# New order and engine choices for the first 330 steps of a linear-attention kernel with a gated convolution

## The chip, the cores and the metric

The kernel runs on one core of a Trainium2 chip. The core has five engines, each with its own queue of instructions that it works through in order: TensorE (PE in the profile; its weight loads are shown as PEld and overlap its matmuls), VectorE (DVE), ScalarE (ACT), GpSimd (POOL) and SyncE (SP), which here only issues transfers. Transfers run on 16 DMA engines and are issued from the queues of SP, GpSimd and ScalarE. [...]

The metric is the device time of the whole program in microseconds (us), as the median of several runs. Lower is better.

## The reference

```python
def _attn_ref(q, k, v, w_phi):          # q, k, v: 8 x 8 x 576 x 64; w_phi: 64 x 128
    def phi(x):
        proj = np.einsum('bhsd,df->bhsf', x, w_phi)
        proj = proj - np.max(np.abs(proj), axis=-1, keepdims=True)
        return np.concatenate([np.exp(proj), np.exp(-proj)], axis=-1)
    q_p, k_p = (phi(q), phi(k))
    kv = np.einsum('bhsf,bhsd->bhfd', k_p, v)
    z = np.sum(k_p, axis=2)
    num = np.einsum('bhsf,bhfd->bhsd', q_p, kv)
    den = np.einsum('bhsf,bhf->bhs', q_p, z)[..., None] + 1e-06
    return num / den

def _moe_ref(x, w_val, conv_w, w_out):  # x: 8 x 576 x 512, the attention's heads side by side
    gate_pre[t] = sum over k < 5 of conv_w[k] * x[t - 4 + k]     # causal, zeros ahead of the start
    gate = 1 / (1 + np.exp(-gate_pre))
    return gate * (x @ w_val) @ w_out
```

The output is 8 x 576 x 512 in float32.

## The kernel before

**Steps.** The work is one list of 1062 numbered steps, made by `build` (from L163) as a loop over the 8 batches. A step is some instructions of one kind on one engine. Within a batch the 18 column blocks of 128 of q and of k are cut into five units (`UNITS`, L24): four of four blocks and a short one of two, here called the first to the fifth block of k or of q. The steps of one batch are these:

- The k and q of batch 0 are loaded as float32 by SP in pieces (`load32`, L520 to L527), transposed on PE (`tp32`, L533 to L536) and copied out of PSUM as bf16 by VectorE or ScalarE (`tc32`, L538 to L544). Batch 1 is loaded by GpSimd as bf16 and transposed on PE (`tp16` and `tc16`, L552 to L562); from batch 2 on, the transposes are DMAs (`xpose`, L564 to L567).
- `kp` and `qm` project k and q with the weights W2 (`proj`, L570 to L578). VectorE takes the largest absolute value of each row (`amax`, L583 to L587; maxima of k go to MK, of q to MQP), and ScalarE takes exp(+x) and exp(-x) of the projected k into KTIL (`kexp`, L593 to L598).
- ScalarE makes exponentials of the maxima of k (`ek`, L600 to L604), GpSimd multiplies V by them (`vs`, L606 to L611), PE sums k's features times V (`st`, L613 to L622), and `kv` copies that out.
- The maxima of q are transposed (`mqt`), negated (`mqr`), spread out into RX by GpSimd (`rx`, L673 to L685) and subtracted inside the second projection of q (`qp`, L687 to L699); ScalarE takes its exponentials into QTIL (`qexp`, L701 to L710).
- `num` multiplies by KV, `nrm` divides (L713 to L741), `xtp` and `xtc` transpose the result, `gate` and `val` are the convolution and the value matmuls (L772 to L792), `tanh` and `gv` gate, `out` multiplies by the output weights, `oev` copies out and `odma` stores.

**The order.** Nothing is scheduled while the kernel runs. Four strings written out by hand at the top of the file set everything: `ORDER` is the order of the steps, and so the order on each engine's queue; `FLEX` has one letter for each step that could go to more than one engine (A for ScalarE, D for VectorE, P for GpSimd); `BANKS` has the PSUM banks of each group of steps, and a group can begin only when the group that had its bank before has been read out; `WARM` and `ZERO` place idle matmuls ahead of positions of `ORDER`. `Plan.follow` (L147 to L156) reads the first three. The durations given with the steps in `build` don't reach the program.

**Idle matmuls.** `warm` (L490) multiplies ones by ones into a bank that nobody reads. `zero` (L493 to L505) adds a product with zeros to a bank that holds a result, which leaves the result as it is.

**The weights of the projection.** `c_w` (L451 to L456) is called while the tiles are made, so it stands ahead of all steps. Its two loads and the load of the convolution's weights are issued from ScalarE's queue; VectorE casts W32 to W2 at L455.

**The hold.** `hold` (L507 to L509) is a one-column copy on GpSimd that reads the last piece of q of batch 0. It stands on GpSimd's queue ahead of the loads of batches 1 and 2 (`load`, L546 to L550), so that they are issued when that piece has landed. `holdx` does the same for later batches.

Of the kernel before, what the change touches and what calls it, by code (L numbers as in the profile page):

```python
# [19 lines left out]
P = 128  # L20
# [15 lines left out]
    "0:5:10:256 13:5:2:512 60:6:1:512 81:1:1:512 87:7:2:512 134:7:1:512 141:7:1:512 "  # L36
)
ZERO = "35:76:7 61:80:5 75:34:1 101:105:1 126:215:8 144:223:1 155:192:4 158:200:1 175:315:6 189:346:1 195:241:2 197:241:2 211:327:1"
# [41 lines left out]
)  # L80
FLEX = (
    "AAAAAADAAADDPPPPDDDDAADDDDDDDDDDDDDAAADAAAADDDDAAADDDAADAAADDADAADDDDADDDDADDDDDDAADADDAAAAAA"
)
BANKS = (
    "037362307001454523232323016701676714232367230101676012354423010145454501013660564675601456745010145450101676767014501454"
# [279 lines left out]
class Emit:  # L365
# [85 lines left out]
    def c_w(self):  # L451
        nc = self.nc
# [37 lines left out]
    def warm(self, bank, n):  # L490
        self.nc.tensor.matmul(self.PS[:, bank, 0:n], self.ONES[:, 0:P], self.ONES[:, 0:n], start=True, stop=True)

    def zero(self, t):  # L493
        w = UNITS[t.u][1] * P
# [345 lines left out]
def kernel(  # L840
# [11 lines left out]
    nc = tc.nc  # L852
# [48 lines left out]
```

## Time and profile before

| | |
|---|---|
| time, median of 3 runs | 216.12 us (216.04 to 216.87) |
| the profiled execution's own time | 215.82 us |
| its span, first to last instruction | 214.1 us |
| PE busy | 195.6 us (91%), 3936 matmuls |
| VectorE busy | 170.3 us (80%) |
| ScalarE busy | 180.3 us (84%) |
| GpSimd busy | 132.6 us (62%) |
| granted TensorE clock, mean | 0.994 |
| moved by DMA | 39.92 MB |

How to read it: a row of the timeline gives start, duration, engine, line of the kernel, operation, output and inputs, and in brackets the idle time of that engine just before it and what ended it. Rows of one kind that follow closely are merged (x2). An engine's name with a q behind it is its queue issuing a transfer. A matmul's duration holds its way through the array, so PE can be busy without being at its peak. The granted clock is the share of full speed that PE was given; it is recorded from 6.6 us on, and where nothing is recorded the views print 1.00.

### The profile page before, as it was taken

How to read it: one execution, taken by the hardware profiler on the slowest of the kernel's cores; microseconds unless marked ns; L12 is line 12 of the kernel's file. 1: busy time of each engine (PE TensorE's matmuls, PEld its weight loads, DVE VectorE, ACT ScalarE, POOL GpSimd, SP SyncE). 2: the span in 40 equal slices, each digit the busy share in tenths (PEclk: the TensorE clock that was granted, in tenths of full speed). 3: DMA queues.
4: the chain of work that ended last, by engine and by line, in shares of the span. 5: the costliest groups of instructions: out<-in, count | busy, mean ns of one | idle time of the engine just before them, and what ended most of it. 6: DMA issues, size and time to landing. Idle time of an engine off the chain costs nothing.

```text
span 214.1 us, 9029 instructions
## 1 busy us (share of the span) xinstructions
PE 195.6 (91%) x3936; PEld 138.9 (65%) x3956; DVE 170.3 (80%) x257; ACT 180.3 (84%) x267; POOL 132.6 (62%) x172
## 2 busy tenths in 40 slices
PE   7968978778999999999999999999999999899990
PEld 5545666566765866767767767568667756787740
DVE  3399999999699979989899789998699897654510
ACT  3799999999999899999899997998988988534351
POOL 3066999995983569944996199804991979110100
PEclk9999999999999999999999999999999999999997
DMA  6999999999999699979996969979952264873166
GB/s 178 363 255 214 308 163 263 183 192 202 147 226 239 107 148 267 271 140 198 222 292 112 167 126 257 169 165 227 276 172 57 78 176 103 107 161 85 52 191 201
DMA packets 49954, 39.92 MB, mean 187 GB/s; under 512 B 34165, under 2 KB 39541, under 8 KB 49914
## 3 DMA queue, kind: packets, MB, share of 16 engines
q1 hardware_dynamic: 43616, 28.65, 58.1%
q0 software_dynamic: 6032, 10.49, 26.5%
q8 instruction: 31, 0.51, 1.0%
q10 hardware_dynamic: 266, 0.21, 0.3%
q14 instruction: 9, 0.07, 0.1%
HBM read 30.48 MB, written 9.44 MB: 187 GB/s over the span
## 4 chain that ended last, share of the span: by engine, by line
PE 53%; ACT 19%; DVE 16%; DMA 4%; issue 4%; SPq 0%; DVEq 0%; ACTq 0%
PE PS L791 12%; PE PS L781 9%; PE PS L813 9%; ACT KTIL L595 8%; ACT QTIL L706 7%; DVE MQP L585 6%; PE PS L719 5%; PE PS L577 4%; PE PS L620 4%; DVE MK L585 3%; DMA KTIL<-in_k_dram 2%; PE PS L693 2%; DMA XT<-XN 2%; DVE XN L740 2%; PE PS L817 2%
## 5 line engine op out<-in xcount | busy, mean ns | idle before, releaser
L595 ACT ACTIVATE KTIL<-PS 128x1024 bf16<-128x1024 f32 (+1 forms) x80 | 72.0, 969 | 2.8 <-PE PS L577 1.4
L610 POOL TENSOR_TENSOR VT<-VN,EK 128x1152 bf16<-128x1152 f32 x32 | 67.9, 2122 | 3.2 <-ACT EK L604 3.1
L706 ACT ACTIVATE QTIL<-PS 128x1024 bf16<-128x1024 f32 x64 | 62.6, 1054 | 1.9 <-PE PS L698 1.5
L682 POOL TENSOR_TENSOR RX<-MQR,ident 128x512 bf16<-128x512 bf16 (+1 forms) x39 | 36.6, 961 | 34.3 <-DVE MQR L670 26.2
L585 DVE TENSOR_REDUCE MK<-PS 128x8 f32<-128x1024 f32 (+1 forms) x40 | 44.2, 1112 | 3.0 <-PE PS L577 1.2
L585 DVE TENSOR_REDUCE MQP<-PS 128x8 bf16<-128x1024 f32 (+1 forms) x40 | 43.6, 1111 | 2.1 <-PE PS L577 1.2
L791 PE MATMUL PS<-XT,WV 128*128 128x288 bf16 x256 | 34.8, 286 | 0.3 <-DVE GV L797 0.2
L797 DVE SCALAR_TENSOR_TENSOR GV<-TH,PS 128x576 bf16<-128x576 bf16 x32 | 23.8, 752 | 10.4 <-PE PS L791 4.7
L813 PE MATMUL PS<-WOUT,GV 128*128 128x512 bf16 x110 | 29.7, 380 | 1.1 <-issue 0.2
L791 PEld LDWEIGHTS <-WV 128*128 128x128 bf16 x256 | 23.8, 98 | 7.9 <-issue 1.4
L785 ACT ACTIVATE TH<-PS 128x576 bf16<-128x576 f32 x32 | 20.4, 664 | 9.0 <-PE PS L781 5.9
L781 PE MATMUL PS<-XT,GW 64*64 64x288 bf16 x640 | 23.1, 285 | 0.8 <-DMA XT<-XN 0.6
L620 PE MATMUL PS<-VT,KTIL 64*128 64x65 bf16 x1152 | 23.1, 191 | 0.6 <-issue 0.4
L740 DVE TENSOR_TENSOR XN<-PS,RCP 128x512 bf16<-128x512 f32 x32 | 22.1, 691 | 1.3 <-DMA XT<-XN 0.3
L620 PEld LDWEIGHTS <-KTIL 64*128 64x128 bf16 x1152 | 20.7, 95 | 3.2 <-issue 2.0
L719 PEld LDWEIGHTS <-QTIL 128*128 128x128 bf16 x512 | 18.3, 97 | 6.4 <-issue 4.1
L719 PE MATMUL PS<-KV,QTIL 128*128 128x65 bf16 x512 | 20.3, 193 | 0.4 <-DVE MQP L585 0.2
L781 PEld LDWEIGHTS <-GW 64*64 64x64 bf16 x640 | 17.8, 106 | 3.2 <-DVE RCP L737 0.7
L634 ACT ACTIVATE OUTS<-PS 128x512 f32<-128x512 f32 x22 | 13.6, 621 | 7.3 <-PE PS L813 6.1
L577 PE MATMUL PS<-W,qT 64*128 64x128 bf16 x288 | 15.0, 217 | 3.9 <-ACT qT L544 1.2
L813 PEld LDWEIGHTS <-GV 128*128 128x128 bf16 x128 | 11.1, 98 | 11.4 <-issue 0.6
L577 PEld LDWEIGHTS <-qT 64*128 64x128 bf16 x288 | 10.6, 94 | 10.2 <-issue 4.8
(79 smaller groups left out, 236.8 us busy)
## 6 DMA issues: line engine op xcount, KB each, us to landing
out_dram<-OUTS SPq DMA_DIRECT2D x32, 256.0 KB, 3.5
VN<-in_v_dram SPq DMA_DIRECT2D x7, 1152.0 KB, 6.7
KQN<-in_q_dram POOLq DMA_DIRECT2D x6, 576.0 KB, 8.1
KQN<-in_k_dram POOLq DMA_DIRECT2D x6, 576.0 KB, 9.5
KTIL<-in_k_dram SPq DMA_DIRECT2D x4, 288.0 KB, 4.3
VN<-in_v_dram POOLq DMA_DIRECT2D x1, 1152.0 KB, 11.9
KTIL<-in_q_dram SPq DMA_DIRECT2D x4, 256.0 KB, 5.2
out_dram<-OUTS SPq DMA_DIRECT2D x14, 64.0 KB, 2.6
```

Source lines behind the costliest of these rows:

```text
L577: nc.tensor.matmul(self.PS[:, t.grp.banks[par], i * P:(i + 1) * P], X[rows, (c0 + i) * P:(c0 + i + 1) * P], self.W2[rows, :], start=True, ...
L585: self.nc.vector.tensor_reduce(o, self.two(t.grp, n * P).rearrange("p a (c f) -> p a c f", f=F), AX.X, ALU.max, apply_absolute_value=True)
L595: self.nc.scalar.activation(self.KTIL[b % 2][:, s, c0:c0 + n, :, :].rearrange("p c a f -> p a c f"), self.two(t.grp, n * P).rearrange("p a ...
L610: nc.gpsimd.tensor_tensor(self.VT[g][:, s, :, 0:D], self.VN[b % 2][:, NC * g:NC * g + NC, :], e.to_broadcast([P, NC, D]), ALU.mult)
L620: nc.tensor.matmul(self.PS[:, t.grp.banks[ab], (s * 2 + x) * E1:(s * 2 + x + 1) * E1], self.KTIL[b % 2][rows, s, J // 2, J % 2, :], self.V ...
L682: self.nc.gpsimd.tensor_tensor(o, *wide(self.MQR[self.mq(b, u)][:, :], self.ident2), ALU.mult)
L706: self.nc.scalar.activation(o, i, AF.Exp, scale=1.0 - 2.0 * s)
L719: nc.tensor.matmul(self.PS[:, t.grp.banks[h // 4], (h % 4) * E1:(h % 4 + 1) * E1], Q[:, s, c % 2, h, (c // 2) * P:(c // 2 + 1) * P], self. ...
L740: nc.vector.tensor_tensor(o.rearrange("p (g h) d -> p g h d", g=ng), n[:, :, :, 0:D], rc.unsqueeze(3).to_broadcast([P, ng, 4, D]), ALU.mult)
L781: self.nc.tensor.matmul(self.PS[o * D:(o + 1) * D, t.grp.banks[par], 0:R], self.GW[r, jj, 4 - m, :], X[r, 4 * a + jj, :, HALO - 8 * s:HALO ...
L791: self.nc.tensor.matmul(self.PS[:, t.grp.banks[par], 0:R], self.WV[:, i, (2 * j + par) * D:(2 * j + par + 2) * D], X[:, 4 * par + i, :, HA ...
L813: nc.tensor.matmul(self.PS[:, t.grp.banks[0], :], GV[:, j, c % 2, (c // 2) * XH:(c // 2) * XH + P], self.WOUT[:, j, c % 2, :], start=(j == ...
```

## The change

- The cast of the projection's weights (`c_w`) goes from VectorE to GpSimd.
- `ORDER` is new up to its position 345 or so; behind that each engine has the steps in the order that it had. All 1062 steps stay. Some of what moves: the first projection of k (step 42) goes ahead of the transposes of k's third block (step 13); on SP the short last piece of q (step 27) goes from ninth to fifth; the exponentials of the first k maxima (step 62) go ahead of the exponentials of k's fifth block (60, 61); on GpSimd the load of batch 1's V (182) goes ahead of the first two row products (86, 87); on SP the duplication of the value weights (164) goes ahead of that of the output weights (427); on GpSimd the loads of batch 3 (429, 431) go behind a V product (206).
- `FLEX`: the copies of k's first, third and fifth block (steps 10, 14, 18) go from ScalarE to VectorE, and the copy of q's second block (step 33) from VectorE to ScalarE.
- `BANKS`: 61 groups get other banks, most of them in batches 0 to 2, some in the last.
- The idle matmuls are placed anew. `WARM` now has items position:bank:n, where n is a size in 256 columns (0 is 128 columns), or position:z step:n for matmuls with zeros; `ZERO` goes.

```diff
 WARM = (
-    "0:5:10:256 13:5:2:512 60:6:1:512 81:1:1:512 87:7:2:512 134:7:1:512 141:7:1:512 "
+    "16:3:1 16:3:1 16:3:0 16:3:0 16:3:0 16:3:0 16:3:0 16:3:0 16:3:0 16:3:0 16:3:0 16:3:0 16:3:0 16:3:0 16:3:0 16:3:0 16:3:0 "
+    "16:3:0 50:2:2 71:7:9 73:z80:1 76:0:1 82:z93:1 85:4:2 88:4:3 125:0:1 175:z232:1 181:6:1 191:4:2 206:0:1 216:2:1 "
 )
-ZERO = "35:76:7 61:80:5 75:34:1 101:105:1 126:215:8 144:223:1 155:192:4 158:200:1 175:315:6 189:346:1 195:241:2 197:241:2 211:327:1"
 ORDER = (
-    "1 2 9 3 4 11 5 6 10 21 22 19 20 13 12 46 25 26 7 8 23 24 14 27 28 42 29 32 30 33 44 49 76 31 15 43 45 47 16 158 159 48 "
-    "77 74 54 57 17 18 160 161 50 52 301 302 75 36 37 55 38 84 80 56 58 85 40 41 303 304 39 87 61 86 60 51 34 182 183 81 35 "
+    "1 2 3 4 5 6 21 22 27 28 19 20 7 8 25 26 9 23 24 11 40 41 10 42 12 13 44 46 14 29 32 158 159 49 43 30 160 161 33 31 47 "
+    "301 302 76 45 15 303 304 77 16 74 182 183 48 54 75 17 36 57 50 18 84 34 53 85 55 87 37 35 51 86 80 56 38 81 39 78 62 93 "
...
 FLEX = (
-    "AAAAAADAAADDPPPPDDDDAADDDDDDDDDDDDDAAADAAAADDDDAAADDDAADAAADDADAADDDDADDDDADDDDDDAADADDAAAAAA"
+    "DADADAAAAADDPPPPDDDDAADDDDDDDDDDDDDAAADAAAADDDDAAADDDAADAAADDADAADDDDADDDDADDDDDDAADADDAAAAAA"
 )
...
-        nc.vector.tensor_copy(self.W2[:, :], self.W32[:, :])
+        nc.gpsimd.tensor_copy(self.W2[:, :], self.W32[:, :])
...
     def warm(self, bank, n):
-        self.nc.tensor.matmul(self.PS[:, bank, 0:n], self.ONES[:, 0:P], self.ONES[:, 0:n], start=True, stop=True)
+        if n == 0:
+            self.nc.tensor.matmul(self.PS[:, bank, 0:P], self.ONES[:, 0:P], self.ONES[:, 0:P], start=True, stop=True)
+        while n > 0:
+            c = min(n, 2) * 2 * P
+            self.nc.tensor.matmul(self.PS[:, bank, 0:c], self.ONES[:, 0:P], self.ONES[:, 0:c], start=True, stop=True)
+            n -= 2
 
     def zero(self, t):
         w = UNITS[t.u][1] * P
-        if t.mode == 0:
-            for _ in range(2):
-                self.nc.tensor.matmul(self.PS[:, t.grp.banks[0], w - P:w], self.NIL[:, :], self.ONES[:, 0:P],
-                                      start=False, stop=True, skip_group_check=True)
-            return
-        c = w // 2 if t.kind == "qp" else w - P
-        for _ in range(1 if w - c > P else 2):
+        c = 2 * P if t.kind == "qp" else P
+        for _ in range(2 * P // c):
             for par in range(2):
                 rows = slice(par * D, (par + 1) * D)
-                self.nc.tensor.matmul(self.PS[:, t.grp.banks[par], c:w], self.NIL[rows, :], self.ONES[rows, c:w],
+                self.nc.tensor.matmul(self.PS[:, t.grp.banks[par], w - c:w], self.NIL[rows, :], self.ONES[rows, 0:c],
                                       start=False, stop=True, skip_group_check=True)
...
         for i, t in enumerate(plan.follow()):
-            for _ in range(zero[i][1] if i in zero else 0):
-                em.zero(plan.tasks[zero[i][0]])
-            for _ in range(warm[i][1] if i in warm else 0):
-                em.warm(warm[i][0], warm[i][2])
+            for to, n in warm.get(i, ()):
+                if to[0] == "z":
+                    for _ in range(n):
+                        em.zero(plan.tasks[int(to[1:])])
+                else:
+                    em.warm(int(to), n)
             if t.fn is not None:
                 t.fn(t)
```

More of the change, by code (lines that the diff above doesn't have):

```diff
@@ L43 @@
 ORDER = (
[36 rows of a table removed]
[36 rows of a table added]
 )
 FLEX = (
-    "AAAAAADAAADDPPPPDDDDAADDDDDDDDDDDDDAAADAAAADDDDAAADDDAADAAADDADAADDDDADDDDADDDDDDAADADDAAAAAA"
+    "DADADAAAAADDPPPPDDDDAADDDDDDDDDDDDDAAADAAAADDDDAAADDDAADAAADDADAADDDDADDDDADDDDDDAADADDAAAAAA"
 )
 BANKS = (
-    "037362307001454523232323016701676714232367230101676012354423010145454501013660564675601456745010145450101676767014501454"
-    "545672012376701230167676745677773567232367232345452301672323232367674545015452343623670101232345454452230145450167676767"
-    "010123014501230167450120167364012345236745454555723014545234567232323010123236745230167232346701422010167454567010121656"
-    "701456701012301670123010167232367674567023677260123230123230167464644501016701670123676745672345232345450123670157672345"
-    "010167452326322345670145670101674545012345012367452345010127452301014545670101765"
+    "672372616101454523232323016723676705012367230101455672345323010123454501452330176470701456745010145450145676723014501454"
+    "501677014576601230167676745677773467232367232345456701676723232367674545014452353623670101232345454452230145450167676767"
+    "010123014501230167450120167365012345236745454555723014545234567232323010123236745230167232346701432010167454567010120656"
+    "701456701012301670123010167232367674567123677260123230123230167475644501016701670123676745672345232345450123670156672345"
+    "010167452345742345670145670101674545012345012367452345010137452301670101452360167"
 )
@@ L857 @@
         for x in WARM.split():
-            i, bank, n, w = x.split(":")
-            warm[int(i)] = (int(bank), int(n), int(w))
-        zero = {}
-        for x in ZERO.split():
-            i, k, n = x.split(":")
-            zero[int(i)] = (int(k), int(n))
-        for i, t in enumerate(plan.follow()):
-            for _ in range(zero[i][1] if i in zero else 0):
-                em.zero(plan.tasks[zero[i][0]])
-            for _ in range(warm[i][1] if i in warm else 0):
-                em.warm(warm[i][0], warm[i][2])
+            i, to, n = x.split(":")
+            warm.setdefault(int(i), []).append((to, int(n)))
+        for i, t in enumerate(plan.follow()):
+            for to, n in warm.get(i, ()):
[4 more added lines that the diff above has]
+                    em.warm(int(to), n)
             if t.fn is not None:
```

68 rows, old and new, of the table ORDER are left out of this document.

## The prediction

> **What bounds the kernel now.** I read the page first, then the busy time of each engine by stretches, cut where the character of the work changes, then the order of time around the start. From the page, and then from the view by stretches (length; busy time and count of PE, weight loads, VectorE, ScalarE, GpSimd; granted clock; DMA share; GB/s):
>
> ```profile
> span 214.1 us, 9029 instructions
> PE 53%; ACT 19%; DVE 16%; DMA 4%; issue 4%; SPq 0%; DVEq 0%; ACTq 0%
> ```
> ```profile
> 0.00:8.02 8.02, 6.46 (x41) 4.16 (x42) 2.00 (x6) 3.01 (x4) 1.78 (x12) 1.00 0.76 230
> 8.02:20.04 12.02, 9.27 (x146) 6.63 (x147) 11.00 (x12) 11.54 (x21) 5.68 (x8) 1.00 1.08 273
> 20.04:36.00 15.96, 13.43 (x342) 9.81 (x343) 15.03 (x23) 15.88 (x22) 15.77 (x15) 1.00 1.14 228
> 36.00:52.00 16.00, 13.08 (x330) 10.29 (x324) 15.35 (x24) 15.61 (x21) 14.69 (x18) 1.00 1.07 208
> 52.00:69.00 17.00, 16.66 (x311) 11.42 (x308) 14.50 (x25) 16.31 (x25) 11.98 (x15) 1.00 1.00 205
> 69.00:207.95 138.95, 135.76 (x2779) 96.33 (x2794) 112.44 (x171) 116.80 (x177) 82.67 (x106) 1.00 0.78 166
> ```
>
> Three stages. To 8.02 us the input loads rule, and ScalarE works 3.01 of 8.02 us. From 8.02 to 52 ScalarE is full: idle 0.48, 0.08 and 0.39 us, 0.95 in all. From 52 on PE is (16.66 of 17.00, then 135.76 of 138.95). The order is kept word for word behind its step 345, which the before reaches near 69 us. So the change can win in two ways: begin ScalarE's full stage sooner, or remove ScalarE's idle time; and what it wins by 52 us starts PE's full stage sooner and reaches the end nearly undiminished.
>
> **The start, row by row.** Timeline of ScalarE, then of PE, VectorE and GpSimd, then a piece of the chain of waits:
>
> ```profile
> 4.93 0.58 ACT L544 CAST kT<-PS 128x512 bf16<-128x512 f32 x1 [0.89 <-PE PS L536]
> 5.86 0.58 ACT L544 CAST kT<-PS 128x512 bf16<-128x512 f32 x1 [0.34 <-PE PS L536]
> 7.46 0.58 ACT L544 CAST kT<-PS 128x512 bf16<-128x512 f32 x1 [1.02 <-PE PS L536]
> 8.02 1.94 ACT L595 ACTIVATE KTIL<-PS 128x1024 bf16<-128x1024 f32 x2
> 10.53 1.02 ACT L595 ACTIVATE KTIL<-PS 128x1024 bf16<-128x1024 f32 x1
> 11.45 0.58 ACT L544 CAST kT<-PS 128x512 bf16<-128x512 f32 x1
> 11.91 1.96 ACT L595 ACTIVATE KTIL<-PS 128x1024 bf16<-128x1024 f32 x2
> 13.73 0.41 ACT L544 CAST kT<-PS 128x256 bf16<-128x256 f32 x1
> 13.98 1.08 ACT L595 ACTIVATE KTIL<-PS 128x1024 bf16<-128x1024 f32 x1
> ```
> ```profile
> 3.81 2.01 PE L536 MATMUL PS<-ident_f,KTIL 128*128 128x128 f32 x8
> 5.61 1.06 PE L491 MATMUL PS<-ONES 128*128 128x512 bf16 x2
> 7.36 0.62 PE L577 MATMUL PS<-W,kT 64*128 64x128 bf16 x16
> 7.91 1.09 PE L536 MATMUL PS<-ident_f,KTIL 128*128 128x128 f32 x8
> 5.16 0.23 DVE L455 CAST W<-W 128x128 bf16<-128x128 f32 x1 [2.36 <-DMA W<-in_w_phi_dram]
> 8.67 0.69 DVE L542 CAST qT<-PS 128x512 bf16<-128x512 f32 x1 [3.29 <-PE PS L536]
> 9.28 2.35 DVE L585 TENSOR_REDUCE MK<-PS 128x8 f32<-128x1024 f32 x2
> 10.65 0.19 POOL L509 CAST HOLD<-KTIL 128x1 bf16<-128x1 f32 x1 [8.26 <-DMA KTIL<-in_q_dram]
> 20.23 2.11 POOL L610 TENSOR_TENSOR VT<-VN,EK 128x1152 bf16<-128x1152 f32 x1 [2.08 <-ACT EK L604]
> 48.88 0.38 POOL L768 COPY XT<-XT 128x224 bf16<-128x224 bf16 x1 [0.97 <-DVE XT L628]
> ```
> ```profile
> 1.67 5.17 DMA KTIL<-in_k_dram
> ```
>
> The first exponential stands at 8.02 because both first projections (L577, 16 matmuls, 7.36) are written behind the transposes of the third block of k, whose load lands at 1.67 + 5.17 = 6.84. Their operands were there before: the copies of the first two blocks end at 5.51 and 6.44, the cast of the weights at 5.39.
>
> **The change, part by part.**
>
> *The cast to GpSimd.* On VectorE it takes 0.23 us and, waiting for its load, closes that queue until 5.39. On GpSimd no row has this shape: from below the one-column cast, 0.19, from above the 224-column copy, 0.38. I take 0.30, being between them by columns: 5.16 + 0.30 = 5.46 (5.35 to 5.54). Behind it on GpSimd stands only the hold, at 10.65 before, so nobody else pays. On the path it costs 0, because the first copy of k ends later, below; a cast 0.5 us dearer would be seen in full.
>
> *PE's order and the copies.* The first projection of k now stands ahead of the third block's transposes. VectorE, free of the cast, copies blocks one, three and five, and ScalarE takes one block of q for them. Block one costs 0.69 there (the row at 8.67) for ScalarE's 0.58: 4.93 + 0.69 = 5.62. PE ends the first eight transposes at 3.81 + 2.01 = 5.82, then runs eight projections; sixteen took 0.62 at full clock, eight then some 0.40, and the clock is lower there (eight transposes took 2.01 us, later 1.09), so I take 0.65: 6.47. ScalarE copies block two meanwhile (5.86 to 6.44) and starts the first exponential at 6.5, ending near 7.4. The second needs block two's projections, which still stand behind the third block: its transposes end near 7.4 (the load at 6.84 and four at 1.09/8 each), then 0.40: ScalarE goes on at 7.85 after waiting 0.4. Steps of a full ScalarE, start to start: one exponential 11.45 - 10.53 = 0.92, one 512-column copy 11.91 - 11.45 = 0.46, one 256-column copy 13.98 - 13.73 = 0.25. Of what the before does between 8.02 and 20.04 (12.02 us) the new order has done one exponential (0.92) by 7.85 and given one 256-column copy away (0.25), and takes one 512-column copy back from VectorE (0.46): 12.02 - 0.92 - 0.25 + 0.46 = 11.31, ending at 19.16, or 0.88 sooner. That keeps the 0.48 us of waits in this stretch; without them it is 1.36. Walking the new order with these steps I found each exponential's matmul done before its turn, so some waits go: I take 1.1.
>
> *VectorE.* It takes three copies (0.69, 0.69, 0.41 at most by ScalarE's own row) and gives one (0.69) and the cast. Two lie in idle time before its first maximum, which moves from 9.28 to about 8.15 (third block's copy 7.45 to 8.14, ahead of it in the order). Against that stands 0.41 later on: about 0.7 sooner at 20 us, and it idles 1.02 of 12.02 there, so it is not the bound.
>
> *GpSimd.* The exponentials of the first k maxima move ahead of the last k exponentials, so its first V product, held until 20.23, can start near 16.5: from 7.85 six exponentials (5.52), five copies (2.30) and a short one (0.25) come first, then its own. GpSimd is full from 20.04 to 36; it gains up to 3.7 us, of which ScalarE lets 1.1 through. The load of batch 1's V moves ahead of two row products (L682), which wait for VectorE's maxima in any case: 0.
>
> *The loads.* On SP's queue the short last q load moves from ninth to fifth, so the hold ends sooner and GpSimd's loads issue sooner:
>
> ```profile
> 2.14 2.09 SPq L525 DMA_DIRECT2D KTIL<-in_q_dram  x3
> DMA to landing us min/median/max: 5.1/5.2/5.3
> QTIL<-in_q_dram POOLq DMA_DIRECT2D x1, 576.0 KB, 6.3
> 19.31 0.61 PE L555 MATMUL PS<-ident,QTIL 128*128 128x128 bf16 x8
> 53.43 3.05 SPq L565 DMA_TRANSPOSE kT<-KQN  x1
> 61.67 0.28 PE L577 MATMUL PS<-W,kT 64*128 64x128 bf16 x4
> ```
>
> Issued second of the three from 2.14 (near 2.8), it lands near 2.8 + 5.3 = 8.1, and the hold ends 2.6 us sooner. Gain: none, for the q load of batch 1, issued behind the hold (10.65 + 0.19), landed 6.3 later, at 17.1, and was first used at 19.31. Cost: between 0 (the rings serve in order of issue) and 2.6 us on the last two q loads (they share); all of q had landed by the hold's 10.65, so 13.3 at worst, and the new order copies them near 13.8 and 14.3 (7.85, five exponentials and three copies). I take 0; with that cover gone, each microsecond late is one of ScalarE's. The V of batch 0 meets these loads sooner too; landing later it takes from GpSimd's gain alone, up to 20.23. Around 40 us the weights' duplications swap places on SP and two loads of batch 3 move behind a V product (2.11): at most 2.1 late, covered by the 8.2 us between the transposes' issue at 53.43 and their use at 61.67, so 0.
>
> *Idle matmuls and banks.* 148 zero matmuls shrink to 8, the others are 15; at the very start 18 short ones stand for ten of the same 2560 columns: 0. The zeros by their line, and PE's timeline:
>
> ```profile
> L504 PE MATMUL PS<-ONES,NIL x148: 216/216/280, 10.3 to 44.0; 64*128 64x128 bf16 x140, 64*128 64x256 bf16 x8
> 10.34 0.96 PE L504 MATMUL PS<-ONES,NIL 64*128 64x128 bf16 x28
> ```
>
> At 0.96/28 = 0.034 us each, 140 fewer free 4.8 us of a PE that is not the bound before 52. What ScalarE waited for them lies inside its 0.95 of idle time, and so do the banks, whose price by itself no row shows: between -0.95 and one more wait of ScalarE, 1.02 by the longest row (7.46). I take 0, nearest to the 0.08 and 0.39 of the two later stretches.
>
> **Sum:** 1.1 us off. The profiled execution (215.82, span 214.1) becomes 214.7; it lies 0.30 under the median 216.12 of the runs shown, which becomes 215.0.
>
> **Rivals.** About 0.5% (1.1 us) is what a measurement can tell from no change.
>
> *The clock closes (other side).* The idle matmuls may hold PE's clock. Stretches of 3.41 us, first two with idle matmuls, third at the end:
>
> ```profile
> 13.43:16.84 3.41, 2.46 (x47) 1.78 (x41) 3.08 (x5) 3.31 (x6) 1.59 (x3) 1.00 1.06 201
> 37.32:40.73 3.41, 2.29 (x48) 1.59 (x45) 3.20 (x5) 3.41 (x5) 3.41 (x5) 1.00 1.03 207
> 207.99:211.40 3.41, 0.95 (x8) 0.26 (x6) 0.00 (x0) 1.19 (x2) 0.00 (x0) 1.00 0.97 306
> 211.40:214.10 2.70, 0.00 (x0) 0.00 (x0) 0.00 (x0) 0.00 (x0) 0.00 (x0) 0.50 0.27 86
> ```
>
> After a stretch with 0.95 of work the clock is 0.50; after 2.29 it is 1.00. Without the 0.7 us of zeros (20 x 0.034 in the first, the same in the second) about 1.6 to 1.8 remain, between the two. A closed stretch doubles its 1.6 us: +1.6 if all lies on the path. One makes 216.6, two 218.2; it decides from the second. Against it: 1.6 is nearer 2.29 than 0.95, and shorter waits pack the real work closer.
>
> [...]
>
> *The clock opens late.* Before, two idle matmuls (5.61, 1.06 us) close the gap ahead of the third block, and the clock opens between 5.8 and 7.9. The new order has 0.65 us of projections there instead. If it opens one stretch of 3.41 us later, the third block's transposes (0.55), the projections (0.40) and four transposes (0.55) double, and the copy that ScalarE takes next comes near 6.84 + 3.0 = 9.9 instead of 7.85 + 0.92 = 8.8: the gain is gone, 216.1. For it: more holes; against: PE still works most of the stretch.
>
> [...]
>
> *More is won.* If ScalarE's remaining waits go too (0.48 + 0.39 + 0.08 to 52, and 17.00 - 16.31 = 0.69 to 69), 0.88 + 0.95 + 0.69 = 2.5: 213.6. For it: GpSimd and PE get slack; against: PE binds from 52.
>
> **How the numbers follow.** Forecast 0.45 (own range 214.4 to 215.6), more won 0.18 (213.6), clock late, or the gain lost in another way, 0.21 (216.1), clock closed 0.16 (216.6 to 218.2). The range 213.4 to 217.2 leaves out most of two closed stretches and little below. Under 215.04 lie half of the forecast and more won: 0.43; over 217.2 most of the closed clock and some unnamed waits: 0.16; between: 0.41.
>
> **What would show it.** First exponential near 6.5 instead of 8.02; what ScalarE had done by 20.04 done by 18.9; hold near 8.1; first V product near 16.5; ScalarE idle under 1 us from 8 to 52; clock 1.00. Wrong, if 128-column transposes are still at half speed after 8 us, if a clock below 1.00 shows before 52, or if ScalarE is 1 us ahead at 20 and no longer at 69.

## The result and the profile after

The changed kernel took 214.79 us (median; 213.98 to 216.43), the kernel before on the same chip 216.94 us. The ratio is 0.9914, 95% interval 0.9885 to 0.9942; the ratios leave out executions that fell into a slower state, so they are not the quotients of the medians. The forecast of 215.0 for 216.12 is a ratio of 0.9948. A second comparison on another chip, told below as g0, gave 0.9948 (0.9915 to 0.9980). So the change wins 0.5 to 0.9%, one to two microseconds. Executions of the changed kernel differ by 2.5 us here and by 3.9 in g0; two things that differ between them turn up below. The profiled execution of the changed kernel took 215.87 us (span 214.1), longer than its median and no shorter than that of the kernel before (215.82, span 214.1). So the two profiles show where time was won and lost, but not the gain of the medians.

The busy time by stretches of the changed kernel, first with the cuts that the prediction used, then three stretches of 3.41 us (length; busy time and count of PE, weight loads, VectorE, ScalarE, GpSimd; granted clock; DMA share; GB/s):

```profile
8.02:20.04 12.02, 10.19 (x125) 6.50 (x128) 11.82 (x16) 11.90 (x22) 6.66 (x8) 1.00 1.09 271
20.04:36.00 15.96, 11.81 (x270) 9.03 (x265) 14.68 (x20) 14.93 (x21) 15.96 (x17) 0.89 1.00 206
36.00:52.00 16.00, 12.85 (x316) 9.55 (x316) 13.40 (x22) 14.68 (x22) 12.73 (x16) 1.00 1.14 229
52.00:69.00 17.00, 16.20 (x290) 10.87 (x284) 15.20 (x26) 16.31 (x24) 12.68 (x15) 1.00 0.93 190
...
25.81:29.22 3.41, 2.23 (x42) 1.73 (x42) 3.05 (x7) 3.41 (x5) 3.41 (x4) 1.00 0.68 141
29.22:32.64 3.42, 3.23 (x100) 3.23 (x101) 2.61 (x4) 2.39 (x5) 3.42 (x5) 0.50 1.24 177
32.64:36.05 3.41, 2.23 (x70) 1.54 (x65) 3.41 (x5) 3.41 (x5) 3.41 (x4) 1.00 0.89 174
```

ScalarE now fills the first stretch (11.90 of 12.02 for 11.54 before). In the next two it has idle time that the kernel before did not have: 1.03 and 1.32 us for 0.08 and 0.39. Between 29.22 and 32.64 the clock is at half. Now the timeline of the changed kernel (start, duration, engine, line, operation, and in brackets the idle time before and what ended it):

```profile
4.99 0.69 DVE L542 CAST kT<-PS 128x512 bf16<-128x512 f32 x1 [2.59 <-PE PS L536]
5.43 0.29 POOL L455 CAST W<-W 128x128 bf16<-128x128 f32 x1 [2.88 <-DMA W<-in_w_phi_dram]
5.77 0.40 PE L577 MATMUL PS<-W,kT 64*128 64x128 bf16 x8
6.21 2.12 ACT L595 ACTIVATE KTIL<-PS 128x1024 bf16<-128x1024 f32 x2
7.38 0.19 POOL L509 CAST HOLD<-KTIL 128x1 bf16<-128x1 f32 x1 [1.66 <-DMA KTIL<-in_q_dram]
7.58 1.21 DVE L585 TENSOR_REDUCE MK<-PS 128x8 f32<-128x1024 f32 x1
18.40 2.12 POOL L610 TENSOR_TENSOR VT<-VN,EK 128x1152 bf16<-128x1152 f32 x1 [3.29 <-DMA VN<-in_v_dram]
20.98 3.81 ACT L706 ACTIVATE QTIL<-PS 128x1024 bf16<-128x1024 f32 x4
51.11 0.29 PE L698 MATMUL PS<-RX,ONES 64*128 64x256 bf16 x2 [1.09 <-issue]
94.92 0.84 PE L620 MATMUL PS<-VT,KTIL 64*128 64x65 bf16 x42 [0.52 <-issue]
```

The row at 20.98 is a good mark for the lead. It begins with ScalarE's third exponential of q (L706). By then both kernels have done the same exponentials. In the kernel before, that one stands here:

```profile
23.11 1.06 ACT L706 ACTIVATE QTIL<-PS 128x1024 bf16<-128x1024 f32 x1
```

So the changed kernel is 2.13 us ahead at the mark, about twice the forecast 1.1. Matching ScalarE's instructions one by one from the end, the lead is 0.31 us at 64 us, 0.42 at 70, and 0.42 at the last. In this profile what is there at 64 us reaches the end, as forecast. But 1.8 us are lost between the mark and 64 us. Two places stand out in the rows: the half clock at 29.22, and the wait of 1.09 us at 51.11 that is put down to "issue", time in which PE waited for nothing that the profile shows.

### The profile page after: what moved, and what is told of

Same layout as the page of the kernel before. It is cut to its first block, busy times and chain, and to the rows that moved or that the text cites. A ratio compares the mean times of both kernels' runs of the same rounds, so it can differ in the third digit from the quotient of the medians.

```text
span 214.1 us, 8769 instructions
## 1 busy us (share of the span) xinstructions
PE 193.5 (90%) x3809; PEld 137.1 (64%) x3829; DVE 170.3 (80%) x258; ACT 178.9 (84%) x265; POOL 133.1 (62%) x173
## 4 chain that ended last, share of the span: by engine, by line
PE 52%; ACT 19%; DVE 8%; DMA 8%; issue 6%; POOL 5%; SPq 0%; ACTq 0%; DVEq 0%; POOLq 0%
PE PS L791 12%; PE PS L813 10%; PE PS L781 9%; ACT QTIL L706 9%; ACT KTIL L595 7%; PE PS L719 6%; DMA VN<-in_v_dram 6%; PE PS L620 4%; POOL VT L610 3%; PE PS L577 3%; DVE MK L585 3%; PE PS L693 2%; PE PS L817 2%; DMA W<-in_w_phi_dram 2%; PE PS L698 2%
## 5 line engine op out<-in xcount | busy, mean ns | idle before, releaser
L706 ACT ACTIVATE QTIL<-PS 128x1024 bf16<-128x1024 f32 x64 | 62.9, 1056 | 1.4 <-PE PS L698 1.3
L813 PE MATMUL PS<-WOUT,GV 128*128 128x512 bf16 x110 | 29.5, 380 | 1.1 <-issue 0.2
L620 PE MATMUL PS<-VT,KTIL 64*128 64x65 bf16 x1152 | 23.9, 194 | 1.6 <-POOL VT L611 0.6
L620 PEld LDWEIGHTS <-KTIL 64*128 64x128 bf16 x1152 | 21.7, 97 | 4.1 <-issue 2.6
L813 PEld LDWEIGHTS <-GV 128*128 128x128 bf16 x128 | 11.2, 98 | 11.4 <-issue 0.6
L577 PE MATMUL PS<-W,kT 64*128 64x128 bf16 x288 | 15.1, 223 | 1.9 <-DVE MQP L585 1.1
```

The lines of the kernel that those rows point to most:

```text
L577: nc.tensor.matmul(self.PS[:, t.grp.banks[par], i * P:(i + 1) * P], X[rows, (c0 + i) * P:(c0 + i + 1) * P], self.W2[rows, :], start=True, ...
L620: nc.tensor.matmul(self.PS[:, t.grp.banks[ab], (s * 2 + x) * E1:(s * 2 + x + 1) * E1], self.KTIL[b % 2][rows, s, J // 2, J % 2, :], self.V ...
L706: self.nc.scalar.activation(o, i, AF.Exp, scale=1.0 - 2.0 * s)
L813: nc.tensor.matmul(self.PS[:, t.grp.banks[0], :], GV[:, j, c % 2, (c // 2) * XH:(c // 2) * XH + P], self.WOUT[:, j, c % 2, :], start=(j == ...
```

## The experiments

All kernels below compute the whole result. Ratios are against the kernel before on the same chip. Each run's text on record stands ahead of what was measured.

**First round: which of the prediction's steps fails.** Four kernels: the hold later again (e1), more idle matmuls in the stretch that came before the half clock (e2), the kernel before without its idle matmuls (e3), and the kernel before with one part of the new order alone (e4).

```diff
-HOLDU = 4                                   # e1, from the changed kernel: reads the piece of q that is issued last
+HOLDU = 2
```

> The changed kernel with one thing undone: the hold on GpSimd reads the piece of q that is issued last before V on SP's queue (the third piece), not the short one, so that GpSimd's four loads are issued near 11 us instead of 7.5. Theory (the early hold lets GpSimd's loads share the rings with batch 0's V, which then lands near 18.3 instead of 13, and the V products are what PE and then ScalarE wait for near 29 to 31 us): the first V product starts near 16.6 instead of 18.40, ScalarE's wait of 1.03 us near 31 shrinks to under 0.4, about 0.8 us faster than the changed kernel, a ratio to the kernel before of 0.986 to 0.989. Rival, the prediction's own price (a later V eats only GpSimd's gain, cost 0): ratio 0.991 as the changed kernel. Second rival (the loads of batch 1 come too late when issued at 11 us): 0.993 or more, with TensorE waiting for batch 1's q or k.

The ratio is 0.9927 (0.9889 to 0.9964): no gain over the changed kernel. Timeline and waits of e1 (its profiled execution, 216.98 us, is one of its longer ones):

```profile
10.92 0.19 POOL L509 CAST HOLD<-KTIL 128x1 bf16<-128x1 f32 x1 [5.26 <-DMA KTIL<-in_q_dram]
16.79 2.12 POOL L610 TENSOR_TENSOR VT<-VN,EK 128x1152 bf16<-128x1152 f32 x1 [0.18 <-ACT EK L604]
```
```profile
PE PS L555 <- DMA QTIL<-in_q_dram: 0.9, 1, 0.9
ACT QTT L709 <- PE PS L698: 0.7, 1, 0.7
```

With GpSimd's loads issued 3.5 us later, V is there before its product and the wait of 3.29 us is gone. So those loads can delay V; with the early hold the first product begins between 16.11 and 18.40 us in ten profiles and waits for V in six of them. But PE now waits 0.9 us for batch 1's q, one of those loads, and ScalarE 0.7 us behind it; e1 has only 0.69 us of lead left at the mark. That wait is what the second rival named. ScalarE's wait near 31 us, which my theory put down to the late V, is still 0.8 us in e1, so the theory falls. Whether the late V costs something smaller is not shown, as e1 brings a wait of its own.

```diff
-... 125:0:1 175:z232:1 ...                  # e2, from the changed kernel: 16 zero matmuls and 3 of 512 columns more
+... 125:0:1 127:z223:4 145:6:6 175:z232:1 ...
```

> The changed kernel with 16 zero matmuls behind the first projection of batch 1's k and three idle matmuls of 512 columns ahead of the first st step, some 1.2 us of TensorE work into the stretch 25.8 to 29.2 us after which the clock fell to 0.50. Theory (the clock closed since the idle matmuls were gone, and a closed stretch costs 1 to 1.6 us): no row below 1.00 between 8 and 53 us, ratio to the kernel before 0.984 to 0.988, and a narrower spread of the times. Rival (the closed stretch lies beside other waits and costs nothing): clock 1.00 and ratio 0.991 or, by the matmuls' own time, up to 0.994.

Slower: 1.0054 (1.0009 to 1.0100), a clear miss. The clock was not at half in this profile, yet PE stood still elsewhere, amid one group of matmuls:

```profile
55.64 0.22 PE L620 MATMUL PS<-VT,KTIL 64*128 64x65 bf16 x3 [2.03 <-issue]
```

```diff
-    "0:5:10:256 13:5:2:512 60:6:1:512 81:1:1:512 87:7:2:512 134:7:1:512 141:7:1:512 "   # e3, from the kernel before
+    "0:5:10:256 13:5:2:512 "
-ZERO = "35:76:7 61:80:5 ..."
+ZERO = ""
```

> The kernel before with all its idle matmuls gone but those ahead of 8 us. Theory (they hold the clock): at least one stretch of 3.4 us at 0.50 between 8 and 45 us, 1 to 3 us slower than the kernel before, ratio 1.005 to 1.014. Rival (they are in the way of real work; 0.96 us of them stands in the chain of waits): clock 1.00 and up to 1 us faster, ratio 0.995 to 1.000.

Ratio 1.0130 (1.0075 to 1.0184). Two stretches of e3 run at half clock, with an open one ahead of them; after them comes another wait of the unknown kind:

```profile
11.07:14.48 3.41, 2.04 (x31) 1.41 (x31) 3.39 (x4) 3.41 (x6) 2.49 (x4) 1.00 1.01 280
14.48:17.89 3.41, 2.19 (x20) 1.45 (x19) 3.41 (x4) 3.19 (x7) 2.11 (x3) 0.50 1.06 195
17.89:21.31 3.42, 3.07 (x28) 1.64 (x27) 2.62 (x4) 3.21 (x9) 1.22 (x2) 0.50 1.17 217
```
```profile
49.49 0.33 PE L748 MATMUL PS<-ident,XN 128*128 128x128 bf16 x3 [1.86 <-issue]
```

The idle matmuls hold the clock: the mean granted clock of e3's six executions is 0.955 to 0.982, that of the 29 of the kernel before on the same chip 0.990 to 1.000. Removing them is not free, but in this profile the half clock is the smaller part. ScalarE was 1.2 us behind the kernel before after the two half-clock stretches, 0.6 at 45 us, and 2.6 behind the wait at 49.49.

```diff
-... 20 13 12 46 ... 27 28 42 29 ... 33 44 49 ...   # e4, from the kernel before: first projections ahead of block three
+... 20 12 42 44 13 46 ... 27 28 29 ... 33 49 ...   # (WARM: "13:5:2:512" goes as well)
```

> The kernel before with one part of the change alone: the projection of k's first block, its copy and its first exponential go ahead of the third block's transposes and copy, and the two idle matmuls that stood there go. The cast stays on VectorE, all copies stay on their engines. Theory (this is the part that wins): first exponential near 6.6 instead of 8.02, ScalarE 0.7 to 1.0 us ahead at 20 us and at the end, ratio 0.995 to 0.997. Rival (the second exponential waits for the third block in any case, and the copies that were done in the meantime now follow): ahead by under 0.3 us at 20, ratio 0.999 to 1.000. Second rival (the clock opens a stretch later without the two idle matmuls): transposes behind 8 us still at half speed, ratio 1.000 or more.

Ratio 0.9985 (0.9952 to 1.0017): nothing measurable, as the first rival had it. The first exponential stands at 6.24, but ScalarE then waits, the longest time for a bank that VectorE still reads, and the lead is 0.14 us at 16 us:

```profile
6.24 1.02 ACT L595 ACTIVATE KTIL<-PS 128x1024 bf16<-128x1024 f32 x1 [0.23 <-PE PS L577]
10.39 1.02 ACT L595 ACTIVATE KTIL<-PS 128x1024 bf16<-128x1024 f32 x1 [0.81 <-DVE MK L585]
```

**What the waits without a releaser are.** The part of the page on DMA queues has this row for the changed kernel:

```profile
q8 instruction: 30, 0.49, 0.9%
```

30 packets of 16,384 bytes go to "instruction". PE has 3809 matmuls and 3829 weight loads in the records, 255 for each packet. Some records are missing (by the page, L813 has 110 matmuls for 128 weight loads), so I took 256 for a packet, an estimate from these counts. I numbered PE's instructions from the start, read the packets' times from the trace, and laid them beside the waits. For the missing records, numbers drift by a few:

```
kernel   PE goes on   number mod 256   last packet landed   PE goes on after
before     95.31           180              94.02                1.28
after      51.11           185              49.82                1.29
after      94.92           180              93.60                1.32
e2         55.64           184              54.24                1.40
e3         49.49           187              47.99                1.50
e3         80.04           185              78.65                1.39
e4         45.98           185              44.75                1.23
e4         53.27           185              51.76                1.51
```

Every such wait ends at the same number modulo 256, within a few, and 1.2 to 1.5 us after a packet has landed. Between the two waits of the changed kernel 7 packets landed and its numbers went on by 1787, again 255 for each. Block ends without a wait have, nearly all, at least that distance (the least in the changed kernel: 1.1 us). So the theory is: PE's instructions arrive in blocks of 256, and where a block lands too late, PE stands still. In the first 60 us of the changed kernel a packet starts up to 4.9 us after PE has passed the block end before (43.99, then 48.85), takes 0.88 to 1.35 us, and needs 1.3 more. Where PE works through 256 short instructions in 4 to 6 us (4.1 from 29.52 to 33.65 in the kernel before), that is not enough. It follows that the mere number of instructions ahead of a place matters, since it says where the blocks end. The second round tests that.

> The changed kernel unaltered, to see what of its first profile comes back. Fetch theory: PE's instructions come in blocks of 256 (30 packets of the instruction queue for some 7640 matmuls and weight loads); where a block lands less than 1.3 us before PE reaches it, PE stands still with no releaser shown, and since the block ends stand at fixed matmuls, so does the wait: 0.4 to 1.6 us near 51 us at the same matmuls of L698, and 0.5 near 95. Clock theory: whether a stretch of low clock shows before 52 us depends on how the 3.41 us grid happens to lie, so the stretch that closed at 29.2 need not come back; a run without it is 0.5 to 1.0 us shorter. Median 214.8 (214.0 to 215.6). Rival: the wait at 51 us was an accident of one execution and is gone, then it is gone in the next three kernels as well, wherever their blocks end.

Ratio 0.9948 (0.9915 to 0.9980). Timeline of g0, the changed kernel again:

```profile
6.06 0.29 POOL L455 CAST W<-W 128x128 bf16<-128x128 f32 x1 [3.51 <-DMA W<-in_w_phi_dram]
6.40 0.40 PE L577 MATMUL PS<-W,kT 64*128 64x128 bf16 x8 [0.84 <-POOL W L455]
6.83 2.14 ACT L595 ACTIVATE KTIL<-PS 128x1024 bf16<-128x1024 f32 x2 [0.65 <-PE PS L577]
21.43 2.90 ACT L706 ACTIVATE QTIL<-PS 128x1024 bf16<-128x1024 f32 x3
94.44 0.85 PE L620 MATMUL PS<-VT,KTIL 64*128 64x65 bf16 x42 [0.65 <-issue]
```

The weights landed 0.63 us later here and held the first exponential; the lead at the mark is 1.68. Half clock returned (28.16 to 31.58, again after a stretch with little work), the wait near 95 too; the one at 51 us did not, as its block landed 1.2 us ahead. The first expectation is half right: the places are fixed, the waits vary (at the place near 95 us 0.52, then 0.65).

```diff
-    "16:3:1 16:3:1 16:3:0 (16 times) ..."   # changed kernel: 2 matmuls of 256 and 16 of 128 columns at the start
+    "16:3:1 16:3:1 16:3:-1 (32 times) ..."  # g1: 32 of 64 columns for the 16 of 128 (n < 0 is 64 columns)
+    "16:3:2 (5 times) ..."                  # g2: 5 of 512 columns for all 18
```

> The same idle columns at the start, cut into 32 matmuls of 64 columns for 16 of 128: 32 more instructions of PE (matmul and weight load), nothing else altered. Fetch theory: every block of 256 now ends 32 instructions earlier in the work. In the changed kernel's profile, PE's own time for the block that then runs from 49.1 is 4.0 us (its own block from 49.8: 5.8), while a fetch there takes 3.3 to 5 us to start, 1 to land and 1.3 more: a wait of 1.5 to 2.2 us near 54 us, at the L620 matmuls, where e2_fill with 37 more had its 2.03, and 0.3 to 1.0 near 50. Slower than the changed kernel by 0.8 to 2.0 us, near 216.2. Rival (the number of instructions does not matter): 214.8, and the waits without a releaser where the changed kernel had them.

Ratio 1.0092 (1.0055 to 1.0129), 218.18 us: 2.95 us slower than g0, for the same idle columns at the start, done in the same time (to 3.8 us in both). Timeline of g1:

```profile
54.09 2.12 PE L792 MATMUL PS<-XT,WV 128*128 128x288 bf16 x16 [2.08 <-ACT EK L605]
95.15 1.10 PE L621 MATMUL PS<-VT,KTIL 64*128 64x65 bf16 x58 [1.90 <-issue]
100.80 0.93 PE L782 MATMUL PS<-XT,GW 64*64 64x288 bf16 x24 [1.42 <-DVE XN L741]
```

Three long waits, 5.4 us together, at the numbers 185, 180 and 179 modulo 256, each 1.27 to 1.29 us after a packet. Two of the rows name a releaser, whose work ended 0.3 and 0.4 us before PE went on; part of these two waits may be its own, but the packets' distance is that of all the others. The one at 54.09 stood in the expectation (near 54 us, 1.5 to 2.2, though it comes behind the `st` matmuls and not among them), the one expected near 50 us did not show, the one at 95 grew from 0.65, and the one at 100.80 is new. The rival falls.

> The same idle columns at the start in 5 matmuls of 512 for the 18: 26 fewer instructions of PE, nothing else altered. Fetch theory: every block ends 26 instructions later in the work; PE's own time for the blocks from 38.2, 44.2 and 50.5 is then 6.0, 6.3 and 5.8 us for 6.6, 5.7 and 5.8 before, so the wait near 51 us falls from 1.1 to 0.5 or less; 0.0 to 0.6 us faster than the changed kernel, near 214.4, and 1.5 us or more faster than the kernel with 32 more. Rival (the number does not matter): 214.8 as the changed kernel, within 0.4, and the wait at the same L698 matmuls.

Ratio 0.9992 (0.9964 to 1.0020): slower than g0 by 0.85 us, where the theory wanted up to 0.6 faster. The waits of g2:

```profile
95.19 0.65 PE L619 MATMUL PS<-VT,KTIL 64*128 64x65 bf16 x29 [1.53 <-issue]
118.49 0.43 PE L780 MATMUL PS<-XT,GW 64*64 64x288 bf16 x5 [0.34 <-issue]
```

The wait at 51 us is gone, as expected, but it was gone in g0 too. I had worked out only the blocks to 57 us; the one at 95 grew by 0.9. The kind was right and the sign wrong, for want of the later blocks.

```diff
-    "16:3:1 16:3:1 16:3:0 (16 times) ... 125:0:1 175:z232:1 ..."          # g3: e2's idle matmuls (fewer zeros),
+    "16:3:1 (4 times) 16:3:2 (3 times) ... 125:0:1 127:z223:2 145:6:6 175:z232:1 ..."   # and 11 fewer at the start
```

> The idle matmuls that e2_fill added between 24 and 29 us, the zeros halved (8 and 3 for 16 and 3), and 11 fewer, wider ones at the start for the same columns, so that from 29 us on PE's instructions have the numbers of the changed kernel. Fetch theory: e2_fill was slow because its 37 more instructions moved the block ends (2.03 us at 55.6, 0.92 at 195.5); with the number as it was these two go and the wait near 51 us comes back: 214.0 to 215.2. If the idle matmuls also keep the stretch at 29 us open, 214.2. Rival (the idle matmuls themselves cost, by PE time or by their bank): near e2_fill, 217 or more.

Ratio 0.9942 (0.9915 to 0.9969), 215.33 us: as g0, and far from e2's 1.0054. So the idle matmuls between 24 and 29 us, of which g3 has 11 for 19, were most likely not what made e2 slow; the number of instructions was. The waits at block ends are 2.3 us in e2's profile and 1.3 in g3's, which is less than half of the difference between the two. No gain over g0 shows either. In this profile, as in e2's, the clock opened only at 10.4 us (in the other nine with this start between 4.3 and 7.4), and the mark stands at 22.49, a microsecond later.

**Third round: a better number, the clock, and two parts undone.**

```diff
-    "16:3:1 16:3:1 16:3:0 (16 times) ..."                                 # h1: 12 matmuls for 18, same columns
+    "16:3:1 (8 times) 16:3:0 (4 times) ..."
-... 125:0:1 175:z232:1 ...                                                # h2: h1, and 6 idle matmuls more
+... 125:0:7 145:6:6 175:z232:1 ...
```

> The same idle columns at the start in 12 matmuls for 18: 12 fewer instructions of PE. Fetch theory: with the need of a fetch by time, as the profiles so far show it, and PE's own time between block ends in the changed kernel, the waits for instructions add up to about 2.6 us in the changed kernel, 2.2 at 12 fewer, 4.8 at 32 more (measured 3.0 us slower) and 2.3 at 26 fewer (measured 0.9 slower, so the sum is good to about 1 us). So 214.9 (214.3 to 215.6) where the changed kernel took 215.2: no longer at 0.5 than it. Rival (more or fewer instructions are slower in either direction only because the start has been altered): between the changed kernel and g2_fewer_instr, 215.6.

Ratio 0.9880 (0.9859 to 0.9902), 214.00 us, the fastest of all: better than expected, and its interval lies below that of g0 and, on its own chip, below that of h3, which has the changed kernel's number of instructions. Its two waits at block ends are short, and none shows near 51 us. They are together no shorter than g0's one of 0.65, so the profiles do not show where h1's gain comes from:

```profile
93.52 0.75 PE L619 MATMUL PS<-VT,KTIL 64*128 64x65 bf16 x36 [0.38 <-issue]
98.89 1.41 PE L780 MATMUL PS<-XT,GW 64*64 64x288 bf16 x38 [0.56 <-issue]
```

> h1 and 6 idle matmuls of 512 columns more between 24 and 29 us, in banks that idle matmuls there use already (0 and 6): from 29 us on PE's instructions have the numbers of the changed kernel. Clock theory: the stretch that closed at 28.2 to 28.9 in four profiles of five with this start (a stretch of low clock cost ScalarE 0.8 to 1.2 us by 36 us, against the one without) stays open: 214.3 (213.7 to 215.2), 0.5 to 1.0 under the changed kernel, and the clock stays 1.00 from its opening to 210 us. Rival (the low stretch costs nothing at the end, because the waits for instructions take it up): 215.2. Second rival (idle matmuls delay the work behind them as much as they save): 215.2 or more with an open clock.

Ratio 0.9896 (0.9880 to 0.9912): within the first theory's time, yet not under h1. The same stretch, 20.04 to 36.00, in h1, then in h2:

```profile
20.04:36.00 15.96, 11.88 (x270) 9.10 (x271) 15.11 (x21) 15.38 (x24) 15.79 (x16) 0.89 1.07 237
```
```profile
20.04:36.00 15.96, 12.19 (x291) 8.29 (x292) 15.30 (x21) 15.72 (x24) 15.76 (x17) 1.00 1.04 241
```

In h2 the clock stays open and ScalarE does 0.34 us more there; the wait near 94 us, 1.12 us in its profile, takes it back.

```diff
-        nc.gpsimd.tensor_copy(self.W2[:, :], self.W32[:, :])     # h3
+        nc.vector.tensor_copy(self.W2[:, :], self.W32[:, :])
-    "DADADAA..."                                                 # h4: FLEX, the first seven letters of the kernel before
+    "AAAAAAD..."
```

> The cast of the weights back on VectorE, all else as changed; the number of PE's instructions is the same. Prediction's step (the cast's place costs or wins nothing by itself; VectorE is freed for the copy of the first block): VectorE now waits for the weights' load, which lands at 5.4 (first profile of the changed kernel) to 6.1 us (second), before its first copy, which stood at 4.99 and 4.59: first exponential at 6.6 to 7.4 for 6.2 to 6.8, ScalarE 0.4 to 0.9 behind the changed kernel at 20 us; median 215.6 to 216.1. Rival (something later binds): the changed kernel's time, 215.2, with the later first exponential.

Ratio 0.9931 (0.9915 to 0.9948), between the two values of the changed kernel. Start and clock of h3:

```profile
5.10 0.23 DVE L455 CAST W<-W 128x128 bf16<-128x128 f32 x1 [2.30 <-DMA W<-in_w_phi_dram]
5.25 0.68 DVE L542 CAST kT<-PS 128x512 bf16<-128x512 f32 x1
6.43 1.02 ACT L595 ACTIVATE KTIL<-PS 128x1024 bf16<-128x1024 f32 x1
```
```profile
20.04:36.00 15.96, 11.76 (x301) 8.62 (x302) 15.45 (x22) 15.96 (x25) 15.94 (x17) 1.00 1.13 225
```

The first exponential is 0.22 us later than in the changed kernel's first profile, 0.40 earlier than in its second: the time at which the weights land decides more than the place of the cast. The place does count at first, as VectorE now copies block one behind the cast. In h1, where the cast began at 5.03, nearly as here, that copy began at 4.92 and the first exponential at 6.11; here they stand at 5.25 and 6.43. By the second exponential, at 7.62 and 7.67, the difference is gone. The last row gives a price of the half clock: with nearly the same program ScalarE works 15.96 us here, 14.93 in the changed kernel; h1 and h2 differ by less.

> The four copies back on the engines of the kernel before (the first, third and fifth block of k on ScalarE, the second of q on VectorE), all else as changed; the number of PE's instructions is the same. Ledger of the prediction: ScalarE takes one copy of 512 columns (0.46, the other being exchanged for q's) and one of 256 (0.25) more; the first lies in its idle time ahead of the first exponential, so it falls 0.3 to 0.7 behind the changed kernel at 20 us; median 215.5 to 215.9. Rival (the engine choice carries the two microseconds of the start, since ScalarE is full from there on): 1.2 or more behind at 20 us and 216.3 or more.

Ratio 0.9936 (0.9904 to 0.9968), no different from the changed kernel; the mark stands at 21.59, 0.16 and 0.61 behind its two profiles. So the copies' engines are worth what the ledger said, or less. With the copies undone 1.52 us of the lead at the mark remain, with the cast undone (h3) 1.93. What remains belongs to the order, the banks and the idle matmuls together: no run takes these apart, and e4's one swap brought 0.14. In h4's profile the lead does not arrive. It is 0.93 us at 64 us and 0.00 at the end, and PE waits 1.14 us at a block end at 94.90.

## Why the prediction was right or wrong

The time and the sign were right. The working was right in the stages and wrong in several terms, which offset each other, so it is in part luck that the sum came so near.

- *The bound.* Right in the stages: ScalarE to 52 us, then PE. "Reaches the end nearly undiminished" held in two profiles (from 64 us to the end 0.31 to 0.42 in the first, 0.90 to 0.77 in g0) and failed in others (1.46 to 0.82 in h3, 0.93 to 0.00 in h4). In h4 0.7 of it goes at PE's wait near 95 us; the rest is unassigned.
- *The cast.* 0.30 forecast, 0.29 measured, and nothing on the path by its place from the second exponential on (h3). Not seen: the weights' load has no slack now. The cast ended at 5.72 and block one's copy at 5.68, and in g0 the cast held the first exponential.
- *PE's order and the copies.* Mis-sized: 1.1 forecast, 2.13 and 1.68 measured at the mark. The first exponential was forecast at 6.5 and came at 6.21 and 6.83. The eight projections took 0.40, not 0.65. The second exponential was forecast at 7.85, after "waiting 0.4". Here it is in the first profile, then in g0:

```profile
7.31 1.02 ACT L595 ACTIVATE KTIL<-PS 128x1024 bf16<-128x1024 f32 x1
```
```profile
7.95 1.02 ACT L595 ACTIVATE KTIL<-PS 128x1024 bf16<-128x1024 f32 x1
```

In the first profile it came early, as the third block landed 0.5 us sooner than in the kernel before; in g0 the forecast held. The lead there was 1.63 and 0.99 us, forecast 1.09 (8.94 less 7.85). What failed in both is the stretch from there to the mark: it added 0.50 and 0.69, forecast next to nothing. ScalarE's waits in it were 0.56 us in the kernel before and 0.12 and 0.00 here, where I had taken away about half. And the exchange of copies, priced at 0.21 more, cost nothing: without its waits the stretch took 13.62 us before, 13.56 and 13.48 here.
- *VectorE.* First maximum forecast at 8.15, measured 7.58 and 8.22.
- *GpSimd.* First V product forecast near 16.5, measured 18.40, since V landed late (16.11 to 18.40 over ten profiles). That it "takes from GpSimd's gain alone" was neither refuted nor shown (e1).
- *The loads.* The hold ended at 7.38 (forecast 8.1). The last q loads cost 0.3 us on PE in one wait, near the 0 taken. "Gain: none" for batch 1's q was wrong: with a later hold PE waits 0.9 us for it (e1).
- *Idle matmuls, "I take 0".* This is the term that failed. Fewer zeros let the clock fall to half for one stretch in five of the eight profiles that have the changed kernel's idle matmuls after the start (the changed kernel, e1, g0, g2, h1; not g1, h3, h4). It costs ScalarE 0.9 to 1.0 us in 20 to 36 us, changed kernel and g0 against h3, and 0.3, h1 against h2. Over the eleven profiles with the new order the lead changes from the mark to 40 us by -0.84 to -0.37 us in the five with the half clock and by -0.14 to 0.41 in the six without: 0.8 apart in the mean. What of it reaches the end is not settled. In g0 the six executions with a mean clock of 0.995 or more took 213.45 to 215.08 us and those with a lower one 215.38 or more; in g2 clock and time show no such order. The rival "the clock closes" named the mechanism and 16 in 100, but at other places (13 and 37 us), and as a loss that decides the sign from the second stretch on; one came, beside a larger gain. Nor was busy time the right measure: stretches of the changed kernel with 2.23 us busy stand on both sides, with 42 matmuls ahead of the half clock and with 70 ahead of an open one.
- *The rival "the clock opens late"* came in two of eleven profiles with this start (e2, g3) at about 1 us on the mark, not the whole gain. Its 0.21, shared with other ways to lose the gain, was an estimate of mine that no row of the kernel before shows. What opens the clock is not settled: after a stretch made of transposes and eight projections the clock opened in h2 (3.98 to 7.39, PE busy 3.41 us) and not in e2 (3.62 to 7.03, busy 3.08).
- *Not in the prediction at all:* the number of PE's instructions. The 140 fewer zeros and 8 more matmuls at the start moved every block end. In the changed kernel's first profile that cost 1.09 us at 51.11.

Two of the three signs that I had named for a wrong prediction did show, a clock below 1.00 before 52 us and a lead at 20 us that shrinks by 69. By these signs the account was wrong where the sum was right. As a ledger against the first profile: 2.1 won, 0.8 lost between the mark and 40 us, where the half clock lies, and 1.1 to the block of instructions, some 0.2 regained or unassigned.

## What to carry to other kernels

Number the instructions of an engine whose waits have no releaser, and look at the queue that brings its instructions: here the ends of its blocks cost 1.6 us in the changed kernel's first profile (1.09 and 0.52) and up to 5.4 in g1's, and how many instructions stand ahead is then a setting like any other, to be tried with wider or narrower idle matmuls. Idle matmuls that look like waste on an engine off the path may hold its clock (0.990 to 1.000 with them, 0.955 to 0.982 without, e3), so price their removal by the stretch that they fill. And when a sum hits the time, still look for its signs: two wrong terms can meet.

## What the runs showed of the hardware

- PE's instructions came in packets, 255 recorded instructions for each (256 is my estimate); PE went on 1.2 to 1.5 us after the packet landed, and 32 more instructions cost 2.95 us (g1). Fewer is not better in itself: 26 fewer cost 0.85 us (g2), 12 fewer won (h1, 0.9880 for 0.9948 and 0.9914, on different chips).
- GpSimd's loads issued 3.5 us sooner delayed a load that SP had issued before them: V's product began at 18.40 for 16.79 (the first profile against e1; six of ten profiles with the early loads show a wait for V). How they delay it, and whether the instruction packets wait for the same reason, was not shown.
- The clock opened between 4.3 and 10.4 us in eleven profiles with one start, and the late openings (e2, g3) were worth a microsecond at the mark. Eight projections took 0.61 us ahead of the opening (h2, at 5.85) and 0.40 behind it (7.43). What fills a stretch enough to keep the clock open stays unsettled.
